# Regrouping the last wo rows of a four-layer decode kernel: 8 and 7 rows, then 2 and 1, with identity matmuls while the last pair is picked

## The chip, the cores and the metric

The kernel runs on one core of one Trainium2 chip. Times are device microseconds of a whole execution. "Span" is the time from the first to the last instruction in the profiled execution; it is about 2 us shorter than the execution's time. One "pair" below is two attention heads. The "granted clock" is the share of the tensor engine's full clock that the trace records as granted; in the traces of the kernel before it is 1.00 or 0.50. PSUM is where the kernel keeps the tiles that its matmuls write.

## The reference

Four layers follow each other, with the weights and caches A, B, A, B. Each is a layer norm of one row of 640 numbers, a query projection to 32 heads of 192, attention over 8192 cached keys and values per head, and an output projection that is added to the row:

```python
q = (x @ wq).reshape(B, Sq, H, Dh)             # Sq = 1, H = 32, Dh = 192
scores = jnp.einsum("bhqd,bhkd->bhqk", q, k_cache) * (Dh ** -0.5)
p = _softmax(scores, axis=-1)
o = jnp.einsum("bhqk,bhkd->bhqd", p, v_cache)
return o.reshape(B, Sq, H * Dh) @ wo           # wo: 6144 x 640
# x = x + layer(layernorm(x)), four times
```

One row against 848 MB of caches and weights: the work is reading them (848.36 MB at the measured 428 GB/s fill the span of 1980.6 us).

## The kernel before

The kernel writes five instruction queues by hand. Transfers are issued in the order of a list `plan`, matmuls in the order of `steps`. 15 of the 16 pairs are projected in three blocks of five pairs; a block of wo is 1920 rows and lies in memory as 15 rows of 640 for each of 128 partitions ("15 rows" below means these). The last pair has 3 such rows of its own. At the end of a layer with `NB[l] > 0` the third block comes in two transfers: 15 - NB rows ahead of the last V, and the last NB behind it. The last V comes as one half and two quarters.

```python
NB = [0, 5, 0, 5]
...
plan.insert(-2, ("wo", l, 2))                  # ahead of the last pair's V
steps += [("busy", l, 16), ("e", l, p - 1)] if NB[l] else [("e", l, p - 1)]
steps += [("v", l, p, 0), ("wc", l, 2)] if NB[l] else [("wc", l, 2), ("v", l, p, 0)]
steps += [("wo", l, 2), ("v", l, p, 1)]
if NB[l]:
    plan.append(("vq", l))                     # V's last quarter
    steps.append(("e", l, p))                  # pick the last pair
    both(("wob", l))                           # the NB rows kept back
...
both(("wol", l))                               # the last pair's 3 rows
```

In these lists `both` appends to `plan` and to `steps`; `wo`, `wob` and `wol` are the block's early rows, its rows kept back and the last pair's rows, `vq` is V's last quarter, and `e` and `wc` pick a pair and turn a block's rows into columns. Identity matmuls into a bank of scores that nobody reads any more (`busy`) fill waits of the tensor engine. The last pair is picked from the PSUM tile by two VectorE instructions and turned into a column by twelve small matmuls; a copy scales it. In layer 3 wo's 640 columns are worked in two halves, `h`, side by side: in the trace before, the two matmuls of such an h pair start within 0.004 us of each other, and pair follows pair after 0.134 us:

```python
def gather(p):                                 # the "e" step
    ...
    for i in range(2 if end else VK):          # end: the last pair
        e = DV.op(... acc[:] <- O[:, i * DH:(i + 1) * DH], pick[:, i:i + 1] ...)
    last["O"] = e
    PE.wait(e, last["TO"], last["TT"])
    for h in range(2):
        if end:
            for c in range(OI):
                e = PE.op(... TB[64 * h:64 * h + 64, c:c + 1], lhsT=acc[:, c:DH:OI], rhs=half[:, h:h + 1] ...)

def project_row(n, w, o, ev_o):                # layer 3
    ...
    PE.wait(ev_o, need(n))                     # o ready, weights landed
    for i in range(k):
        for h in range(2):
            e = PE.op(... YR[32 * h:32 * h + 1, :], lhsT=o[:, i:i + 1], rhs=t3[:, i, h * HD:(h + 1) * HD] ...)
```

## Time and profile before

| kernel before | |
|---|---|
| median of the first 3 executions | 1982.81 us (1982.56 to 1983.79) |
| span of the profiled execution | 1980.6 us |
| read from memory, mean rate | 848.36 MB, 428 GB/s |
| V's last quarter landed (last of its sixteen records) | 1974.19 us |
| last wo rows landed | 1977.23 us |
| V's landing to the end of the span | 6.42 us |
| **last landing to the end of the span** | **3.38 us** |

A landing is the last of the sixteen records that the trace has of a transfer's arrival (for V's last quarter they run from 1968.95 to 1974.19 us). The program moves the same bytes before and after the change (848.36 MB read in both profiles), so the time of the last landing belongs to the stream of transfers, and what follows it is what the change can shorten.

### The profile page before, as it was taken

The page shows a single profiled execution, that of the slowest core. Times are in us where ns is not written, and L with a number is a line of the kernel's source. Part 1 is how long each engine was busy: PE and PEld are TensorE (multiplying, and loading weights), DVE is VectorE, ACT ScalarE, POOL GpSimd, SP SyncE. Part 2 cuts the span into 40 slices and gives each one's busy share as a digit, 9 for nine tenths or more (in the row PEclk, how much of TensorE's full clock was granted, in tenths as well). Part 3 has the DMA queues.
Part 4 walks back from the last instruction along what each step waited for, and adds up shares of the span by engine and source line. Part 5 has one row for each costly group of instructions (what it writes and reads, how often), then busy time and mean ns, then how long its engine had stood idle before and what let it go on. Part 6 is the DMA issues. An engine that isn't in the chain of part 4 may idle for free.

```text
span 1980.6 us, 13743 instructions
## 1 busy us (share of the span) xinstructions
PE 1288.7 (65%) x8245; PEld 146.4 (7%) x3159; DVE 1201.3 (61%) x1376; ACT 139.9 (7%) x462; POOL 4.5 (0%) x23
## 2 busy tenths in 40 slices
PE   3567476666466666665785675666676766666658
PEld 0001001000200100100020010010002001001001
DVE  3567467467166656566745565665764775665756
ACT  0000000000000000000010000000000100000000
POOL 0000000000000000000000000000000000000000
PEclk9787776778587777777787778877886878777779
DMA  9999999999999999999999999999999999999998
GB/s 413 435 435 429 430 430 433 436 428 429 436 430 431 430 435 433 427 433 432 426 412 431 426 429 432 431 428 432 431 430 428 435 431 435 431 432 432 431 432 367
DMA packets 26786, 849.25 MB, mean 429 GB/s; under 512 B 3042, under 2 KB 3044, under 8 KB 3812
## 3 DMA queue, kind: packets, MB, share of 16 engines
q1 hardware_dynamic: 26580, 848.38, 99.6%
q8 instruction: 45, 0.74, 0.2%
q14 instruction: 17, 0.14, 0.0%
q10 hardware_dynamic: 144, 0.00, 0.0%
HBM read 848.36 MB, written 0.00 MB: 428 GB/s over the span
## 4 chain that ended last, share of the span: by engine, by line
DMA 67%; PE 19%; DVE 12%; ACT 1%; issue 0%; SPq 0%
DMA pool<-in_B_k_cache_dram 27%; DMA pool<-in_A_v_cache_dram 22%; DMA pool<-in_A_k_cache_dram 13%; DVE pool L596 10%; PE S L58 10%; DMA pool<-in_B_v_cache_dram 6%; PE OY L58 5%; PE OY L675 3%; DVE acc L694 1%; ACT p_sb L633 1%; DVE s_sb L618 1%; PE S L609 1%; PE OY L535 0%; DVE m_bf L620 0%; PE QM L623 0%
## 5 line engine op out<-in xcount | busy, mean ns | idle before, releaser
L596 DVE TENSOR_TENSOR pool<-pool,q_sb 128x3072 bf16<-128x3072 bf16 x512 | 861.1, 1753 | 235.0 <-DMA pool<-in_B_k_cache_dram 139.5
L58 PE MATMUL S<-pool,ident 128*128 128x512 bf16 x2944 | 793.4, 428 | 17.0 <-DVE pool L596 15.4
L705 PE MATMUL TB<-acc,small 128*1 128x192 f32 x240 | 81.8, 491 | 212.0 <-DVE acc L694 212.0
L58 PE MATMUL OY<-pool,p_sb 128*16 128x512 bf16 x1920 | 198.1, 488 | 0.0
L693 DVE TENSOR_SCALAR acc<-OY,small 128x192 f32<-128x192 f32 x64 | 26.7, 418 | 281.1 <-PE OY L58 251.6
L609 PE MATMUL S<-pool,ident 128*128 128x512 bf16 x128 | 62.3, 487 | 203.9 <-DVE pool L596 203.8
L675 PE MATMUL OY<-pool,p_sb 128*16 128x512 bf16 (+1 forms) x1216 | 146.3, 489 | 67.4 <-DMA pool<-in_A_v_cache_dram 59.9
L694 DVE SCALAR_TENSOR_TENSOR acc<-OY,small,acc 128x192 f32<-128x192 f32 x424 | 177.1, 418 | 14.9
L618 DVE TENSOR_REDUCE s_sb<-S 128x64 f32<-128x512 f32 x128 | 88.0, 688 | 68.0 <-PE S L58 68.0
L524 ACT ACTIVATE q_sb<-QM 128x192 bf16<-128x192 f32 x60 | 19.9, 331 | 949.8 <-PE QM L518 949.8
L716 ACT ACTIVATE rows<-TB,small 1x192 bf16<-1x192 f32 x120 | 43.2, 405 | 590.6 <-PE TB L705 590.6
L689 DVE RECIPROCAL small<-TB 1x2 f32<-1x2 f32 x64 | 11.2, 175 | 94.9 <-PE TB L648 75.2
L633 ACT ACTIVATE p_sb<-s_sb,small 64x128 bf16<-64x128 f32 x128 | 55.7, 435 | 160.8 <-DVE small L627 160.0
L609 PEld LDWEIGHTS S<-pool,ident 128*128 128x128 bf16 x128 | 12.9, 101 | 683.1 <-DVE pool L596 589.1
L648 PE MATMUL TB<-small,ones 128*1 128x2 f32 x120 | 11.4, 165 | 74.1 <-ACT p_sb L633 74.1
L675 PEld LDWEIGHTS OY<-pool,p_sb 128*16 128x16 bf16 (+1 forms) x1216 | 38.9, 106 | 213.4 <-issue 137.2
L623 PE MATMUL QM<-ident,m_bf 128*64 128x64 bf16 x128 | 14.1, 217 | 54.4 <-DVE m_bf L620 53.8
L705 PEld LDWEIGHTS TB<-acc,small 128*1 128x1 f32 x240 | 19.7, 101 | 308.1 <-DVE acc L694 280.7
L627 DVE TENSOR_REDUCE small<-QM 128x1 f32<-128x64 f32 x64 | 14.4, 225 | 35.2 <-PE QM L623 35.2
L518 PEld LDWEIGHTS QM<-rows,one_b 1*64 1x64 bf16 x120 | 6.2, 100 | 344.2 <-issue 338.4
L535 PE MATMUL OY<-oT,pool 128*128 128x1 bf16 x675 | 28.6, 178 | 1.9 <-ACT oT L581 1.9
L535 PEld LDWEIGHTS OY<-oT,pool 128*128 128x128 bf16 x675 | 27.8, 131 | 3.8 <-ACT oT L581 2.5
(74 smaller groups left out, 218.3 us busy)
## 6 DMA issues: line engine op xcount, KB each, us to landing
pool<-in_B_k_cache_dram SPq DMA_DIRECT2D x28, 6144.0 KB, 38.3
pool<-in_B_v_cache_dram SPq DMA_DIRECT2D x28, 6144.0 KB, 34.5
pool<-in_A_v_cache_dram SPq DMA_DIRECT2D x27, 6144.0 KB, 27.6
pool<-in_A_k_cache_dram SPq DMA_DIRECT2D x34, 3072.0 KB, 20.3
pool<-in_A_k_cache_dram SPq DMA_DIRECT2D x14, 6144.0 KB, 36.4
pool<-in_A_v_cache_dram SPq DMA_DIRECT2D x10, 3072.0 KB, 14.2
pool<-in_B_k_cache_dram SPq DMA_DIRECT2D x8, 3072.0 KB, 22.6
pool<-in_A_wo_dram SPq DMA_DIRECT2D x6, 2400.0 KB, 21.8
```

Source lines behind the costliest of these rows:

```text
L58: return t.add_instruction(mybir.InstMatmult(name=t.bass.get_next_instruction_name(), engine=mybir.EngineType.PE, ins=[t.lower_ap(rhs), t. ...
L524: lambda a: a.activation(q_sb[i][:], QM[:, 0:DH], ACT.Copy), e, last["q"][i], bank=QMu)
L535: e = PE.op(lambda t, i=i, c=c, f=y_first[0], fin=n[0] == "wol" and i == k - 1: t.matmul(YB[:, c:c + 1], lhsT=t3[:, i, c:D:DC], rhs=o[:, i ...
L596: e = DV.op(lambda v, d0=d0: v.tensor_tensor(k3[:, :, d0:d0 + QD], kin[:, :, d0:d0 + QD], q_sb[qi][:, d0:d0 + QD].unsqueeze(1).broadcast_t ...
L609: t.matmul(S[:, :], lhsT=ident[:], rhs=k3[:, :, d0:d0 + R], start=True, stop=fin) if d0 == 0 else
L618: lambda v, u=u: v.tensor_reduce(s[:, u * JU:(u + 1) * JU], SP_[u][:].rearrange("p (j r) -> p j r", r=R), AX.X, ALU.add), ev_S[p, u], last ...
L633: ev_p[p] = AC.op(lambda a, h=h, r=r: a.activation(p_sb[par][r, :, h], s[r, :], ACT.Exp, bias=negm[par][r, 0:1], accum_out=l_col[par][r, h ...
L675: t.matmul(o, lhsT=x, rhs=y, start=f, stop=fin) if c == 0 else
L693: v.tensor_scalar(acc[:], O[:, 0:DH], pick[:, 0:1], None, ALU.mult) if i == 0 else
L694: v.scalar_tensor_tensor(out=acc[:], in0=O[:, i * DH:(i + 1) * DH], scalar=pick[:, i:i + 1], in1=acc[:], op0=ALU.mult, op1=ALU.add)), e if ...
L705: e = PE.op(lambda t, h=h: t.matmul(TB[96:97, C_O + h * DH:C_O + (h + 1) * DH], lhsT=half[:, h:h + 1], rhs=acc[:], start=True, stop=True), ...
L716: last["TO"] = last["row_written"] = AC.op(lambda a, h=h: a.activation(orow[:, o0 + h * DH:o0 + (h + 1) * DH], TB[96:97, C_O + h * DH:C_O ...
```

## The change

Its intent is to have V's last quarter land earlier, by moving two rows of the wo block from in front of it to behind it, and to let the last matmuls begin before the very last row is there. The identity matmuls were meant to keep the tensor engine's clock up. `woe` is the last pair's third row.

```diff
-    NB = [0, 5, 0, 5]
+    NB = [0, 5, 0, 7]
...
             both(("wol", l))
+            if l == 3:
+                both(("woe", l))
...
-            if n[0] == "wol":
+            if n[0] in ("wol", "woe"):
                 r0 = o["wol"] * PD
+                a, b = (0, OI) if l < 3 else (0, OI - 1) if n[0] == "wol" else (OI - 1, OI)
                 return SP.op(lambda s: s.dma_start(
-                    rows[:], w["wo"][r0:r0 + PD].rearrange("(p i) n -> p (i n)", p=P)),
-                    *free, sem=semOL, inc=16)
+                    rows[:, a * D:b * D], w["wo"][r0:r0 + PD].rearrange("(p i) n -> p (i n)", p=P)[:, a * D:b * D]),
+                    *free, sem=semOL if n[0] == "wol" else semOE, inc=16)
...
                 last["O"] = e
+                if end and l == 3:
+                    busy(3)
                 PE.wait(e, last["TO"], last["TT"])
...
+                elif n[0] == "woe":
+                    last["oTl"] = ev_y = project_row(n, rows[:, (OI - 1) * D:], oTl[:, OI - 1:], last["TTn"])
+                elif l == 3:
+                    project_row(n, rows[:, 0:(OI - 1) * D], oTl, last["TTn"])
```

## The prediction

> **What bounds the kernel now.** I read the page first. The engine mix matters less than the transfers: the chain of work that ended last is two thirds DMA, and all 40 slices but the last show the DMA engines at nine tenths or more.

> ```profile
> DMA 67%; PE 19%; DVE 12%; ACT 1%; issue 0%; SPq 0%
> ...
> DMA  9999999999999999999999999999999999999998
> GB/s 413 435 435 429 430 430 433 436 428 429 436 430 431 430 435 433 427 433 432 426 412 431 426 429 432 431 428 432 431 430 428 435 431 435 431 432 432 431 432 367
> ```

> The reader is to see that 848 MB at about 430 GB/s are the time. The change moves no byte out of the program and touches only layer 3's end, so all it can alter is the last few microseconds. The second view is the chain in order of time from 1966 us of the 1980.6 us span (start, us, what):

> ```profile
> 1936.94 37.25 DMA pool<-in_B_v_cache_dram
> 1974.19 0.04 issue
> 1974.23 0.85 PE OY L675 x16
> 1975.09 0.02 issue
> 1975.11 0.43 DVE acc L693
> 1975.54 0.02 issue
> 1975.56 0.43 DVE acc L694
> 1975.99 0.04 issue
> 1976.04 0.89 PE TB L701 x12
> 1976.93 1.20 PE OY L567 x16
> 1978.13 0.02 issue
> 1978.15 0.43 ACT pool L760
> ```

> The last quarter of V lands at 1974.19; after it comes a serial chain: its 16 matmuls, two VectorE instructions that pick the diagonal, 12 small matmuls that turn it into columns, 16 matmuls with wo (10 of the block kept back, 6 of the last pair's rows), the copy to a row, and the store. The third view, DMA issues from 1925 us on (KB each, us from issue to landing), says what lies behind that V quarter:

> ```profile
> pool<-in_B_v_cache_dram SPq DMA_DIRECT2D x2, 1536.0 KB, 35.6
> pool<-in_B_wo_dram SPq DMA_DIRECT2D x1, 800.0 KB, 38.7
> rows<-in_B_wo_dram SPq DMA_DIRECT2D x1, 480.0 KB, 7.6
> ```

> The timeline has the issues of the last two at 1937.41 and 1969.62, so the wo block lands at 1976.1 and the last rows at 1977.2. The chain needs them at 1976.86 and about 1977.4 (starts in the timeline below). Before the change the tail's last data are thus ready 0.7 and 0.2 us early, while V's last quarter is waited for: the tensor engine had finished its filler matmuls at 1973.43 and stood until 1974.23.

> ```profile
> 1971.97 0.39 PE L427 MATMUL S<-ident 128*128 128x512 bf16 x1
> 1972.19 1.24 PE L58 MATMUL S<-ident 128*128 128x512 bf16 x5
> 1974.23 0.82 PE L675 MATMUL OY<-pool,p_sb 128*4 128x384 bf16 x16 [0.80 <-DMA pool<-in_B_v_cache_dram]
> 1976.04 0.89 PE L701 MATMUL TB<-small,acc 128*64 128x1 f32 x12 [0.98 <-DVE acc L694]
> 1976.86 0.84 PE L567 MATMUL OY<-pool,oT 128*1 128x320 bf16 x10
> 1977.53 0.57 PE L567 MATMUL OY<-rows,oTl 128*1 128x320 bf16 x6
> ```

> [...]the sixteen landing records of V's last quarter run from 1968.95 to 1974.19, so a landing is its slowest engine's. On that engine successive landings are 3.68 us (1536 KB), 1.89 (800 KB) and 1.15 (480 KB) apart: bytes in order at 417 to 423 KB per us. [...]the new pieces have 1280 B per partition. The trace's packets took 149 ns for 3840 B, 244 for 6400 and 464 for 12288, a line of about 7 ns plus 0.037 ns per byte; 1280 B is my extrapolation, near 54 ns. [...]granted clock was 1.00 in every half microsecond from 1964 to 1978 and 0.50 after the last matmul. The gap of about 1 us during the picking cost no clock in this execution.

> **Part by part.**
> (1) The wo block kept back grows from 5 rows of 15 to 7; the part sent ahead of V's last three pieces shrinks from 10 rows to 8. Two rows are 128 x 2 x 640 x 2 B = 320 KB; at the slow engine's pace (3.68 us for 1536 KB) that is 0.77 us. V's last quarter lands at 1974.19 - 0.77 = 1973.42; the wo block still ends at 1976.08, as the bytes ahead of its end are the same. Will the tensor engine be there at 1973.42? The early wo matmuls fall from 20 to 16. An h pair runs side by side: 10 matmuls took from 1976.86 to 1977.53, 0.134 us per pair. Two pairs fewer end the work before the wait 0.27 us sooner, near 1973.1 instead of 1973.43. So V is still waited for, by 0.3 us.
> (2) From V's landing the serial part is unchanged. In the old trace 1974.19 to 1976.86 is 2.67 us; moved up it reaches the wo block at 1976.09. But that block lands at 1976.08: with the usual 0.04 us from landing to start, 1976.12. The 0.77 us gained is here 0.74.
> (3) 7 rows instead of 5 after it: 7 pairs x 0.134 = 0.94 us, to 1977.06, instead of 0.67. So 0.27 us is given back, and 0.47 us of gain is left.
> (4) The last rows come as 2 and 1. The first two pairs, 0.27 us, run to 1977.33; their data (320 KB after 1976.08, 0.78 us) have landed by 1976.86. The last row, 160 KB, ends where the old 480 KB ended, 1977.23, plus 8 more packets per engine at 7 ns and one more count: 1977.3. With 0.04 us to start, 1977.34, just where the tensor engine arrives. The old last pair began 2 x 0.134 after 1977.53, at 1977.80. Gain: 0.46 us, less perhaps 0.05 for a weight load that no longer hides behind the pair before (the timeline shows the first wo weight load and matmul starting together after a wait). I take 0.42 us. Without the split the whole 480 KB, landed at 1977.23, would start at 1977.27 and need three pairs, ending 0.2 us later; that is what the split is worth.
> (5) Three identity matmuls while the pair is picked. They are issued after V's 16 and take about 0.1 + 3 x 0.213 = 0.74 us (from the six that took 1971.97 to 1973.43). V's matmuls occupy about 0.64 us before the next can follow, and VectorE then needs until 1.8 us after landing. The three are through near 1.6 us after V's landing, ahead of it: no delay, about 0.2 us to spare. They save nothing where the clock is at 1.00.[...]
> Copy and store are unchanged. Sum: -0.77 (V earlier) + 0.03 (wo block's landing) + 0.27 (two rows moved behind) + 0.05 (last row) = -0.42[...]: -0.5 us of 1982.8, or 0.03%.

> **Rivals.**
> A: the last bytes become the wait. In (2) and (4) the tensor engine arrives within 0.03 us of both landings. If the 1280 B packets run at half of the expected rate, the last landing moves by 8 x 54 ns = 0.43 us and the gain is gone: 1982.8. For it: no packet between 640 B and 3840 B is in the trace near the end. Against: the line through three sizes, and 640 B at 32 ns in the store's two packets, on or near that line.
> B: V's earlier landing is not used. If the tensor engine arrived at the wait only at 1973.9, the gain would shrink by half a microsecond and the two moved rows cost 0.27: 1982.8 to 1983.0. For it: fillers and the early wo block must all pass first. Against: the 0.80 us wait ahead of V's matmuls now.
> C: the identity matmuls collide with the picking, holding the 12 small ones back. For it: only about 0.2 us to spare, and if the clock were already halved three of them would take 1.3 us. That would add up to 0.5 us. Against: full clock throughout that stretch.
> D: nothing can be seen, as executions of one kernel differ by more: the three times of before spread over 1.2 us (1982.56 to 1983.79), two to three times the expected gain. Likely for a median of three.

> **Range and chances.** From 1982.81 less 0.5: 1982.3 us. The uncertainty is mostly the spread of runs, about 0.6 us to either side, plus 0.4 us for A to C; I take 1981.4 to 1983.3. 2% is 40 us, six times the 6.4 us from V's landing to the end of the span; nothing in the diff could move that much unless the transfer order of earlier layers changed, and the instruction order shows it unchanged up to the last five transfers. Faster by over 2%: 0.003; slower: 0.003.

> **What would show each step.** V's last quarter landing 0.7 to 0.8 us earlier against the end of the span, with a shorter wait ahead of its 16 matmuls (1); 14 wo matmuls starting about 0.74 us earlier, with a DMA wait of a few hundredths at most (2, 3); 4 and then 2 with the last rows, the final pair about 0.45 us earlier, perhaps with a DMA wait (4); three identity matmuls ended before VectorE does and clock 1.00 to the last matmul (5). The prediction is wrong if V's landing moves and the end doesn't, which would name A or C; if the landing doesn't move, the per-engine order in (1) was wrong.

Its sum came to -0.5 us. The terms left in it give -0.42 (-0.77, +0.03, +0.27 and +0.05); a term of -0.1 for the clock is cut together with the argument for it, and the -0.5 and the 1982.3 us still contain it. That each of the sixteen landing records is one engine's is the author's reading; the trace doesn't name the engine.

## The result, and the profile after

The changed kernel took 1982.13 us (median of 6, 1981.83 to 1983.93), the kernel before in the same rounds and the earlier three 1983.24 us (median of 6, 1982.22 to 1986.6). The ratio is 0.9994 with a 95% interval of 0.9981 to 1.0007: the same. Ratios are the mean time of one kernel's fast runs over that of the other's, so not quite the ratio of these medians. The predicted 1982.3 us lies 0.2 us off, but such a hit says little, as the spread of runs is larger than the whole effect. What can be checked is the tail in the trace. The profiled execution happens to be the slowest of the six (1983.93), and all its times are about 1 us later than before.

This is the chain in order of time from 1966 us of the changed kernel (start, us, what):

```profile
1937.43 37.95 DMA pool<-in_B_v_cache_dram
...
1975.43 0.85 PE OY L678 x16
...
1976.30 0.43 DVE acc L696
...
1976.76 0.43 DVE acc L697
...
1977.23 0.89 PE TB L706 x12
1978.12 0.00 issue
1978.12 1.54 PE OY L570 x20
```

Against the old chain, the wo matmuls are 20 instead of 16 and take 1.54 us instead of 1.20; everything from V's landing to them is as it was. From the changed kernel's DMA issues from 1925 us on (KB each, us to landing):

```profile
pool<-in_B_wo_dram SPq DMA_DIRECT2D x1, 1120.0 KB, 40.2
rows<-in_B_wo_dram SPq DMA_DIRECT2D x1, 320.0 KB, 8.1
rows<-in_B_wo_dram SPq DMA_DIRECT2D x1, 160.0 KB, 8.1
```

The 800 KB block has become 1120 KB, and the 480 KB are now 320 and 160. The landing records put V's last quarter at 1975.38, the block at 1978.08 and the last row at 1979.26. V is thus 3.88 us ahead of the last landing, where it was 3.04. The changed kernel's timeline, tensor engine lines:

```profile
1975.43 0.82 PE L678 MATMUL OY<-pool,p_sb 128*4 128x384 bf16 x16 [1.12 <-DMA pool<-in_B_v_cache_dram]
1976.18 0.39 PE L430 MATMUL S<-ident 128*128 128x512 bf16 x1
1976.41 0.59 PE L58 MATMUL S<-ident 128*128 128x512 bf16 x2
1977.23 0.89 PE L706 MATMUL TB<-small,acc 128*64 128x1 f32 x12 [0.23 <-DVE acc L697]
1978.12 1.11 PE L570 MATMUL OY<-pool,oT 128*1 128x320 bf16 x14
1979.07 0.57 PE L570 MATMUL OY<-rows,oTl 128*1 128x320 bf16 x6
```

The three identity matmuls end at 1977.00 (1976.41 + 0.59), the picking at 1977.18. The 14 wo matmuls start at 1978.12, 0.04 us after their block's landing. Seven pairs later, at 1979.07, the last rows begin; the last pair starts at 1979.34, 0.08 us after the landing of its row. The end of the span comes 2.88 us after that landing; before, 3.38. So the tail is **0.50 us shorter** by this measure. From V's landing it is 0.34 us longer (6.76 against 6.42), as two rows were put behind it: the gain is that V lands 0.84 us earlier against the last landing.

The 0.50 us is a little too large for what the end gains, as the split was also expected to put the last landing itself about 0.05 us later. The landing of the wo block doesn't have this flaw: the bytes ahead of its end are the same before and after. From it to the end took 4.53 us before (4.48 and 4.52 in two runs below that end as before) and 4.06 us after (4.07 in a second execution): **0.41 to 0.47 us shorter**.

### The profile page after: what moved, and what is told of

It reads as the page before. It is cut to its first block, busy times and chain, and to the rows that moved or that the text cites. A ratio compares the mean times of both kernels' runs of the same rounds, so it can differ in the third digit from the quotient of the medians.

```text
span 1982.1 us, 13748 instructions
## 1 busy us (share of the span) xinstructions
PE 1288.6 (65%) x8248; PEld 146.4 (7%) x3160; DVE 1201.2 (61%) x1376; ACT 139.9 (7%) x462; POOL 4.5 (0%) x23
## 2 busy tenths in 40 slices
DMA  9999999999999999999999999999999999999998
## 4 chain that ended last, share of the span: by engine, by line
DMA 67%; DVE 17%; PE 15%; ACT 1%; issue 0%; SPq 0%
DMA pool<-in_B_k_cache_dram 27%; DMA pool<-in_A_v_cache_dram 20%; DVE pool L599 15%; DMA pool<-in_A_k_cache_dram 14%; PE S L58 6%; DMA pool<-in_B_v_cache_dram 6%; PE OY L58 5%; PE OY L678 3%; DVE acc L697 1%; ACT p_sb L636 1%; DVE s_sb L621 1%; PE S L612 0%; DVE m_bf L623 0%; PE OY L538 0%; PE QM L626 0%
## 5 line engine op out<-in xcount | busy, mean ns | idle before, releaser
L599 DVE TENSOR_TENSOR pool<-pool,q_sb 128x3072 bf16<-128x3072 bf16 x512 | 861.1, 1753 | 229.5 <-DMA pool<-in_B_k_cache_dram 133.5
L58 PE MATMUL S<-pool,ident 128*128 128x512 bf16 x2944 | 789.5, 425 | 19.5 <-DVE pool L599 17.6
L58 PE MATMUL OY<-pool,p_sb 128*16 128x512 bf16 x1920 | 202.7, 498 | 0.0
```

The lines of the kernel that those rows point to most:

```text
L58: return t.add_instruction(mybir.InstMatmult(name=t.bass.get_next_instruction_name(), engine=mybir.EngineType.PE, ins=[t.lower_ap(rhs), t. ...
L599: e = DV.op(lambda v, d0=d0: v.tensor_tensor(k3[:, :, d0:d0 + QD], kin[:, :, d0:d0 + QD], q_sb[qi][:, d0:d0 + QD].unsqueeze(1).broadcast_t ...
```

## The experiments

Each kernel gives the reference's numbers. In the texts "tail" is the end of the span minus the last landing, and "V to end" the end of the span minus the landing of V's last quarter.

### Each part alone

Only the division into 8 and 7 (first diff line alone, on the kernel before):

```diff
-    NB = [0, 5, 0, 5]
+    NB = [0, 5, 0, 7]
```

> Only the 8/7 division of the wo block; last rows in one transfer, no identity matmuls. Measure: end of span minus the landing of the last wo transfer (before 3.38 us, changed kernel 2.88). Theory (V earlier, then the last landing is the wait): V lands 0.77 us earlier relative to the last landing (3.8 us ahead of it instead of 3.0), the last rows start about 0.04 us after their landing and need three pairs: tail 3.1 us, so 0.27 us of the gain. Rival (V's earlier landing is not used): tail 3.4 or more. Time within 1 us of before either way.

Measured: V 3.82 us ahead of the last landing, V to end 7.02 us, tail 3.20 us; time 1983.17 us, ratio 0.9998 (0.9981 to 1.0014). From its timeline:

```profile
1976.77 1.11 PE L567 MATMUL OY<-pool,oT 128*1 128x320 bf16 x14
1977.99 0.26 PEld L567 LDWEIGHTS OY<-rows,oTl 128*1 128x1 bf16 x6 [0.46 <-issue]
1978.03 0.57 PE L567 MATMUL OY<-rows,oTl 128*1 128x320 bf16 x6
```

The 14 matmuls were issued by about 1977.71 (1976.77 + 7 x 0.134), the last rows landed at 1977.89 and their first matmul started at 1978.03. The theory holds: the last landing is now the wait. The restart cost 0.14 us instead of the 0.04 that I had put in, hence 3.20 and not 3.1. This part alone gains 0.18 us of tail (0.12 against the two runs that follow, whose tail is 3.32).

Only the last rows in transfers of 2 and 1 (the changed kernel with the block back at 10 and 5 and without the identity matmuls):

```diff
-    NB = [0, 5, 0, 7]
+    NB = [0, 5, 0, 5]
...
-                if end and l == 3:
-                    busy(3)
```

> Only the last rows in transfers of 2 and 1; the block stays 10/5, no identity matmuls. Theory: worth nothing alone, as the last rows had landed 0.2 to 0.3 us before they were needed: tail from last landing to the end 3.3 to 3.4 us, V to end 6.4 us as before. Rival (the split itself shortens the end): tail about 3.1.

Measured: tail 3.32 us, V to end 6.42; time 1983.46 us, ratio 0.9999 (0.9984 to 1.0014). Alone it gains nothing: V to end is as before to the hundredth.

Only the identity matmuls, added to the kernel before:

```diff
                 last["O"] = e
+                if end and l == 3:
+                    busy(3)
                 PE.wait(e, last["TO"], last["TT"])
```

> Only the three identity matmuls added to the kernel before. Theory: they end before the picking does (about 0.2 us to spare) and the clock was full anyway: V to end 6.42 us and tail 3.38 us as before, within 0.05. Rival (they collide with the picking): V to end 6.6 to 6.9. Rival (they keep the clock up): the same in an execution with full clock, so it shows only where the clock falls before the last matmul.

Measured: V to end 6.41 us, tail 3.32; the three end 1.62 us and the picking 1.79 us after V's landing; time 1982.96 us, ratio 0.9997 (0.9982 to 1.0012). They neither cost nor save anything here. The tails of 3.32 in this run and the last one, against 3.38 of the kernel before, with the same V to end, show how well this measure repeats: the last landing itself shifts by some hundredths against V's.

The changed kernel without the identity matmuls:

```diff
-                if end and l == 3:
-                    busy(3)
```

> The changed kernel without the three identity matmuls. Theory: V to end 6.76 us and tail 2.88 us as with them, if the clock stays full to the last matmul[...].

Measured: V to end 6.76 us, tail 2.89, clock 1.00 to the last matmul; time 1983.56 us, ratio 0.9998 (0.9983 to 1.0013). Against the run with the division alone, the split of the last rows is worth 0.26 us from V's landing (7.02 to 6.76) once V lands early; the tail says 0.31 (3.20 to 2.89), but in it the last landing comes 0.05 us later against V. In this execution the identity matmuls are worth nothing.

### How many rows to keep back

The changed kernel with another number in place of the 7 (one execution each, so only their traces are compared):

```diff
-    NB = [0, 5, 0, 7]
+    NB = [0, 5, 0, 6]      # and 8, and 10
```

> The changed kernel with 6 of 15 rows kept back instead of 7. Two limits meet: the tensor engine arrives 2.7 us after V's landing and the wo block's landing 1.15 us before the last. With 6 rows V lands 3.45 us before the last landing, the wo matmuls start 0.74 us before it and 6 + 2 pairs of 0.134 us bring the last pair to 0.33 us after it: tail from last landing to end about 3.14 us (7 rows: 2.88). Rival (the tail is set by the last landing alone): 2.9.

Measured: V 3.48 us ahead of the last landing, tail 3.07 us (one execution, 1982.98 us).

> The changed kernel with 8 rows kept back. The wo matmuls can't start before their landing, 1.1 us before the last, so the extra row costs its pair: last pair 0.23 us after the last landing, tail about 3.04 us; the tensor engine now waits some 0.4 us for the wo block. Rival (later is still better, V earlier): 2.8 or less.

Measured: V 4.24 us ahead, tail 2.99 us (one execution, 1982.41 us). Its timeline shows the wait for the block:

```profile
1976.38 1.25 PE L570 MATMUL OY<-pool,oT 128*1 128x320 bf16 x16 [0.34 <-DMA pool<-in_B_wo_dram]
```

> The changed kernel with 10 rows kept back. By the same sum two more pairs than with 8: last pair 0.50 us after the last landing, tail about 3.31 us, wait for the wo block about 1.1 us. Rival (later is still better): 2.8 or less. It may also show that the tensor engine no longer waits for V, as V lands before the fillers end: then V to its first matmul is more than 0.04 us.

Measured: V 5.01 us ahead, tail **4.43** us where the sum gave 3.31 (one execution, 1985.1 us). V's matmuls started 0.09 us after its landing, behind the fillers. This one missed, and its timeline shows why:

```profile
1975.76 0.89 PE L706 MATMUL TB<-small,acc 128*64 128x1 f32 x12 [0.23 <-DVE acc L697]
1977.73 2.29 PE L570 MATMUL OY<-pool,oT 128*1 128x320 bf16 x20 [1.09 <-DMA pool<-in_B_wo_dram]
1979.81 1.01 PE L570 MATMUL OY<-rows,oTl 128*1 128x320 bf16 x6
```

The six matmuls of the last rows take 1.01 us instead of 0.57. The record of granted clock falls from 1.00 to 0.50 at 1978.33, 0.6 us into the wo matmuls, after the wait of 1.09 us for the block. To see whether the idle time took the clock, the wait was filled:

```diff
                 elif n[0] == "wob":
+                    if l == 3:
+                        busy(4)
                     last["oT"] = freed[("wo", l, 2)] = (project_row if l == 3 else project)(
```

> 10 rows kept back, with four identity matmuls more in the wait for the wo block (the run with 10 rows stood 1.1 us there and lost half of its clock 0.6 us into the wo matmuls: tail 4.43 instead of 3.31). Theory[...]: clock 1.00 to the last matmul, tail 3.3 us. Rival (ten rows are slow for another reason): 4.4 again.

Measured: tail 3.26 us (one execution, 1982.77 us), clock 1.00 to the last matmul:

```profile
1975.47 0.39 PE L430 MATMUL S<-ident 128*128 128x512 bf16 x1
1976.47 1.52 PE L570 MATMUL OY<-pool,oT 128*1 128x320 bf16 x20
1977.82 0.57 PE L570 MATMUL OY<-rows,oTl 128*1 128x320 bf16 x6
```

So tails of 3.07, 2.88, 2.99 and, with full clock, 3.26 us belong to 6, 7, 8 and 10 rows kept back. With fewer than 7 the tensor engine arrives late because V does; with more it waits for the block and then has more of it to do. Seven is the best of those tried. No version here was shown to beat the changed kernel.

### Identity matmuls: too many, and none

Six instead of three while the pair is picked:

```diff
-                    busy(3)
+                    busy(6)
```

> The changed kernel with six identity matmuls instead of three while the last pair is picked. Three ended 0.18 us before the picking; three more take 0.64 us, so the twelve small matmuls start 0.45 us later: V to end 7.2 us instead of 6.76, tail 3.3 instead of 2.88. Rival (the tensor engine takes them beside the rest at no cost): 2.9.

Measured: V to end 7.04 us, tail 3.17 (one execution, 1982.05 us). From its timeline:

```profile
1974.24 1.24 PE L58 MATMUL S<-ident 128*128 128x512 bf16 x5
1975.42 0.89 PE L706 MATMUL TB<-small,acc 128*64 128x1 f32 x12
```

The small matmuls no longer wait for VectorE (no bracket); they wait for the identity matmuls and start 2.20 us after V's landing instead of 1.85. The collision is real, but 0.35 us and not 0.45, and 0.07 us of it vanish in the wait for the block. Three fit, six don't. That this execution was among the shortest in time shows again that a single time can't rank these kernels.

None in the tail, neither the three nor the six ahead of V's last quarter:

```diff
-                        if l == 3:
-                            busy(6)
...
-                if end and l == 3:
-                    busy(3)
```

> The changed kernel without any identity matmuls in the tail: neither the three nor the six ahead of V's last quarter. Theory: the tensor engine idles some 2.5 us before V and 1 us after it[...], so the clock halves before the end: V to end 7.3 to 8.5 us instead of 6.76.[...] Rival (fillers don't matter): 6.76.

Measured: V to end 7.67 us, tail 3.79 (one execution, 1983.7 us). The granted clock fell to 0.50 at 1977.05:

```profile
1973.91 0.82 PE L676 MATMUL OY<-pool,p_sb 128*4 128x384 bf16 x16 [2.03 <-DMA pool<-in_B_v_cache_dram]
1976.61 1.64 PE L570 MATMUL OY<-pool,oT 128*1 128x320 bf16 x14
1978.03 1.01 PE L570 MATMUL OY<-rows,oTl 128*1 128x320 bf16 x6
```

The last six take 1.01 us again. In this execution, without the fillers, V to end is 0.91 us longer (7.67 against 6.76). The run with six identity matmuls in the picking was still fast at its end (its last six took 0.57 us). The six ahead of V were in the kernel before already; whether the three add anything for the clock stays open, as no execution without the three alone was seen to lose its clock ahead of its last matmul. The kernel before came close: its clock fell at 1978.42, 0.3 us after its last matmul ended.

Busy time as the profile counts it doesn't tell when the clock falls. The 3.41 us ahead of the two drops held 2.10 us of busy matmul time (10 rows kept back; longest pause 1.09 us) and 2.16 us (no fillers; 1973.64 to 1977.05). Stretches of the same length with less kept their clock: 2.08 us in the kernel before (1964.77 to 1968.18) and 1.66 us in the run without fillers (1970.22 to 1973.64).

### Time again, and what the stream of transfers depends on

The changed kernel once more, in 5 rounds:

> The changed kernel once more, for the time and for the tail in another execution. Tail from last landing to the end 2.9 us, V to end 6.75 us whatever the span; median 0.3 to 0.8 us under the kernel before. If the tail repeats to 0.05 us while spans differ by over 1 us, the spread of times lies before the last landing.

Measured: 1982.20 us (median of 5), the kernel before 1983.67 us (median of 9), ratio 0.9994 (0.9982 to 1.0007); V to end 6.74 us and tail 2.87 with a span of 1980.6 us. The tail repeats to 0.02 us while the spans of the two profiled executions differ by 1.5 us. In these two the difference in time therefore lies ahead of the last landing.

The sixteen landing records of V's last quarter are 5.24 us apart in the kernel before and 6.10 in the changed one (5.42 in its second execution). In the kernel before the distance grew in steps through the first two layers (1.14 us at 22 us, 4.24 at 780, 5.22 at 845) and was back to 2.42 us at 1027. The 45 packets of 16 KB on its queue q8, which the page calls "instruction", took a median of 1.07 us each. To see whether the reading of instructions drives the engines apart, 2048 one-element memsets per layer went to the nearly idle gpsimd engine (4.5 us busy in the page of the kernel before):

```diff
+            for i in range(2048):
+                spared[0] = PO.op(lambda g, i=i: g.memset(spare[:, i % 64:i % 64 + 1], 0.0), ...)
```

> The changed kernel with 2048 memsets of one element in each layer on the idle gpsimd engine, 8192 in all, whose results nobody uses. Question: why do the sixteen DMA engines drift 4 to 6 us apart by the end, so that a landing is the slowest one's? Theory: each 16 KB packet of the instruction queue (45 of them, about 1.07 us each) holds up the one engine it falls on. [...]time 2 to 5 us longer, spread at the end 6 to 9 us, tail after the last landing still 2.9. Rival (the engines differ in their own rate): packets rise, time and spread stay. Control: mean of VectorE's products stays at 1.75 us.

Measured: 2016.12 us (median of 4), ratio 1.0164 to the kernel before (1.0148 to 1.0179), tail 2.86 us. The control held: the mean VectorE product stayed at 1753 ns. Neither theory had the size. That a packet holds up the engine it falls on was not shown. The 16 KB packets stayed 45; the new ones are of 8 KB on another queue that the page calls "instruction". Here is that queue in the page of the kernel before, then of this run:

```profile
q14 instruction: 17, 0.14, 0.0%
```

```profile
q14 instruction: 81, 0.66, 0.1%
```

Among all records of 8 KB packets on that queue there are 24 before and 87 here, at about 0.31 us each. Landings near 2010 us lay 12.2 us apart. So the added instructions did cost time: about 34 us (1982.20 to 2016.12) for 8192 memsets and 63 packets, on average 63 B a memset. If all fell on one engine they would take it 20 us (63 x 0.31, an estimate), which is not enough. Nor was the time lost mainly where the packets came: while the memsets ran in the first, second and fourth layer, the rate was 432, 430 and 429 GB/s (30 to 125, 525 to 620 and 1540 to 1626 us), against 434, 431 and 433 in the same stretches of the second execution above. In the third (1037 to 1120) it was 401 against 432, and in stretches without memsets 422 against 431 (620 to 1000) and 423 against 429 (1120 to 1500). Which engine served the packets was not recorded, and the layers' starts may also have been delayed; the cause stays open.

## Why the prediction was right

The time can't tell (rival D), so what was right shows in the trace alone. The size of the effect was right there because each wait was taken from the path that sets the end, and what was saved ahead of V was charged again behind it.

- **Step 1, V earlier by 0.77 us.** Right: V's lead over the last landing grew from 3.04 to 3.88 us, 0.84, of which 0.05 was expected from the later last row. The tensor engine still waited for V, for 1.12 us in the first profiled execution, 0.21 in the second and 0.12 in the run without the three identity matmuls; 0.3 was predicted, but a wait that varies so much hits it only by luck. Rival B fell.
- **Step 2, the block's landing limits the start.** Right: the wo matmuls start 0.04 us after it, 2.74 us after V (2.70 predicted). The runs with 6 and 8 rows show the two sides of this balance.
- **Step 3, 0.27 us given back by two more rows.** Right: seven pairs took 0.95 us (0.94 predicted).
- **Step 4, the last row lands as the tensor engine arrives.** Right: the last pair starts 0.08 us after that landing, at the even pace of the pairs before it, so it didn't wait. The 1280 B packets took 55 ns (54 predicted), so rival A fell. The value of the split was under-sized: 0.26 us instead of 0.2, because the restart without it cost 0.14 us and not 0.04, and with it the last pair started 0.08 us after the landing and not 0.04. One reading was loose: the old last rows' first matmul is at 1977.53 in the lines shown, 0.3 us after their landing; the "about 1977.4" is that of its weight load.
- **Step 5, identity matmuls.** Right in that three fit, with 0.17 us to spare (0.2 predicted), so rival C fell for three and holds for six. The sum behind it doesn't add up: 0.64 and 0.74 make 1.4 us, not the 1.6 that it gives; measured were 0.75 and 0.82, which with 0.04 to start make the 1.62. The 0.1 us for the clock was the author's estimate and was not shown; that the clock can fall to 0.50 in such a tail was, by the runs with 10 rows (tail 4.43 us, 3.26 with the wait filled) and without fillers (3.79).
- **Rival D** is what the times show. The sum of -0.42 us, for the end against the stream of transfers, is matched by -0.41 to -0.47 from the wo block's landing; the tail's -0.50, and -0.51 in the second execution, have the later last landing in them. The medians differ by 1.1 and 1.5 us, which the interval of about 2.5 us to either side doesn't tell from 0.5 or from nothing.

## What to carry to other kernels

When bytes are moved behind a transfer that is waited for, look for the point where three arrivals meet: the engine after its serial chain, the data moved, and the last byte; here the end was later on either side of it (tails of 3.07 and 2.99 us with 6 and 8 rows, 2.88 with 7). Splitting the very last transfer paid here only once that transfer had become the wait (0.26 us; nothing before). Measure such changes from a landing that has the same bytes ahead of it, or from the last one, to the end, which repeated to 0.06 us where whole executions differ by more than the effect, and fill waits with matmuls only as far as the next real operand leaves room (three fitted, six made V to end 0.28 us longer).
